# Re-ordering the first phase of a sliding-window attention and FFN kernel

## The chip, the core and the metric

The kernel runs on one core of a Trainium2 chip. The metric is the device time of one execution in microseconds (us), lower is better. Engine names are those of the profile: PE is the matrix engine, PEld its weight loads, DVE the vector engine, ACT the scalar engine, POOL the general engine, SP the engine that only issues DMAs. An "issue" on SP or POOL is the instruction that starts a DMA.

## The reference

Eight batches, eight heads, 576 positions, 64 elements to a head; a causal window of 64 positions. The attention's output becomes 4608 tokens of 512 elements, which go through a multiplicative FFN. All inputs and the output are float32.

```python
scores = scale * np.matmul(q, k.transpose(0, 1, 3, 2))
mask = (rel >= 0) & (rel < window)                # rel = query - key position, window = 64
attn = softmax(where(mask, scores, -1e9))
x = (attn @ v).transpose(0, 2, 1, 3).reshape(B * S, H * D)       # 4608 x 512
a = x @ w1 ; b = x @ w2                           # 512 -> 1024 each
out = ((a * b) @ w3) @ w_out                      # 1024 -> 1024 -> 512
```

## The kernel before

**The attention** is cut into 96 units of work, 12 to a batch (3 stretches of 192 queries, 4 pairs of heads). `tick(u)` issues, in this order, `scores(u)` (2 matmuls into PSUM, one exponential on ACT, then 2 or 4 mask instructions on POOL, lines 262 and 264), every second tick one `transposes` for the next batch, `values(u - 2)` (4 matmuls with V, two logarithms and an exponential on ACT, two multiplications on DVE that write the ring buffer `xT`), and then the loads and casts for later batches that fall on this tick. `LAG = 2` is the distance between the scores of a unit and its values.

**q and k** of a batch are loaded in four DMAs each by SP into a buffer `stage` (4 buffers, shared with the weights), cast to float16 into `k16`/`q16`, and turned by `transposes`: per call 6 transposing matmuls into one PSUM tile `tp` (one buffer) and a copy out of it, by DVE for k, by ACT and then DVE for q. **V** is loaded by DMAs that POOL issues and that cast on the way, as six blocks of 128 rows at rows 0, 64, 128, 256, 320 and 448; neighbouring blocks overlap by 64 rows, so 768 rows are read for 576.

**The FFN** works on 9 groups of 512 tokens. A group is eight `ffn_ab` (8 matmuls of 512 columns, an ACT copy and a DVE multiplication each) and four `ffn_o` (8 matmuls, a DVE copy, a store issued by SP at once). w3 and w_out are multiplied once into `wc_sb` ("the fold"): for each of 8 slices of w3 `fold` casts it on POOL, turns it with 8 transposing matmuls into `tp` and copies it out on DVE, and `fold_mm` multiplies (8 matmuls, one ACT cast).

**The order** is written out by the program: all instructions of one engine run in the order in which the code issues them. First come the loads and transposes of batch 0, the loads and casts of w1 and w2 and the k and q of batch 1; then 14 ticks alone; then the parts of each group, with ticks between them by due times:

```python
need = [12 * B if g == NG - 1 else 12 * g + 4 * -(-(GT - 64 * g) // 192) for g in range(NG)]
...
slots.append((w, lo + (hi - lo) * (i + 1) / len(part) + LAG))
```

`need[g]` is the number of units that group g reads, so a group begins right behind the tick that holds the values of its last unit. Group 0 has the eight fold steps between its `ffn_ab` and its `ffn_o`. At each third of a batch SP copies a row of logarithms to `lnsum`; at the end DVE checks them all, and a branch follows that is not taken.

Of the kernel before, what the change touches and what calls it, by code (L numbers as in the profile page):

```python
# [144 lines left out]
def kernel(  # L145
# [122 lines left out]
    def values(u):  # L268
# [28 lines left out]
        if j == NJ - 1:  # L297
            n = 2 * (3 * b + si)
            nc.sync.dma_start(out=lnsum[n:n + 2, :], in_=y[0:P:D].rearrange("a j n -> a (j n)"))
            del lns[b, si]  # L300

    NU = 12 * B

    def tick(u):
# [4 lines left out]
        if u % 2 == 0 and b + 1 < B:  # L309
            transposes(b + 1, "kq"[r // 6], r % 6 // 2)  # L310
        if 0 <= u - 2 < NU:
            values(u - 2)
        if 3 <= r < 9 and b + 1 < B:
            load_v(b + 1, r - 3)
        if r in (2, 5) and b + 2 < B:
            load_qk(b + 2, "kq"[r == 5])
        if r in (0, 2) and 0 < b + 1 < B:
            cast_qk(b + 1, "q", r // 2, pool_cp)
        if r in (7, 9) and b + 2 < B:
            cast_qk(b + 2, "k", (r - 7) // 2, pool_cp)  # L320
# [32 lines left out]
    w3s = {}
    wo = {}

    def load_w12(dc):
        st = sb.tile([P, 2, 1152], FP32, name="stage", bufs=4)
        for i, src in enumerate((moe_w1, moe_w2)):
            nc.sync.dma_start(out=st[:, i, 0:DF], in_=src[dc * P:(dc + 1) * P, :])
        dve_cp(w1_sb[:, dc, :], st[:, 0, 0:DF])  # L360
        pool_cp(w2_sb[:, dc, :], st[:, 1, 0:DF])

    def load_wo():
        wo[0] = sb.tile([P, 8, DM], FP16, name="ab", bufs=3)
        for half in range(2):
            st = sb.tile([P, 2, 1152], FP32, name="stage", bufs=4)
            for i in range(2):
                e0 = half * 4 + i * 2
                nc.sync.dma_start(out=st[:, i, 0:DF].rearrange("p (e m) -> p e m", e=2),
                                  in_=moe_w_out[e0 * P:(e0 + 2) * P, :].rearrange("(e p) m -> p e m", p=P))  # L370
                pool_cp(wo[0][:, e0:e0 + 2, :], st[:, i, 0:DF].rearrange("p (e m) -> p e m", e=2))

    def load_w3(fc):
        st = sb.tile([P, 2, 1152], FP32, name="stage", bufs=4)
        for i in range(2):
            nc.sync.dma_start(out=st[:, i, 0:DF], in_=moe_w3[(fc + i) * P:(fc + i + 1) * P, :])
        w3s[fc] = st

    def fold(fc):

        st = w3s[fc - fc % 2]
        w3 = sb.tile([P, DF], FP16, name="t2k", bufs=4)
        pool_cp(w3, st[:, fc % 2, 0:DF])  # L383
# [126 lines left out]
```

## Time and profile before

| | us |
|---|---|
| median of 3 runs | 381.17 (381.16 to 382.66) |
| profiled execution, its own time | 382.25 |
| its span, first to last instruction | 380.7 |
| PE busy in the span | 282.8 (74%) |
| DVE, ACT, POOL busy | 209.4, 209.7, 213.1 (55%, 55%, 56%) |
[...]

A busy share is a mean over the whole span. The kernel has a first phase, in which weights, q, k and V have to come in, and a steady phase of one FFN group after the other; the table does not say which of the two a given microsecond of idle PE lies in.

### The profile page before, as it was taken

How to read it: one execution, taken by the hardware profiler on the slowest of the kernel's cores; microseconds unless marked ns; L12 is line 12 of the kernel's file. 1: busy time of each engine (PE TensorE's matmuls, PEld its weight loads, DVE VectorE, ACT ScalarE, POOL GpSimd, SP SyncE). 2: the span in 40 equal slices, each digit the busy share in tenths (PEclk: the TensorE clock that was granted, in tenths of full speed). 3: DMA queues.
4: the chain of work that ended last, by engine and by line, in shares of the span. 5: the costliest groups of instructions: out<-in, count | busy, mean ns of one | idle time of the engine just before them, and what ended most of it. 6: DMA issues, size and time to landing. Idle time of an engine off the chain costs nothing.

```text
span 380.7 us, 5928 instructions
## 1 busy us (share of the span) xinstructions
PE 282.8 (74%) x1922; PEld 163.9 (43%) x1922; DVE 209.4 (55%) x374; ACT 209.7 (55%) x491; POOL 213.1 (56%) x354
## 2 busy tenths in 40 slices
PE   0220555298536688998998998998998998998970
PEld 0120444044323344554554555974554554554430
DVE  7643355146313226666777778575787676555350
ACT  1220476246223234685987888674996996673300
POOL 6022798747462335477699699466889665250000
PEclk9999999999878889999999999999999999999996
DMA  9999989754963203699099499649926723002020
GB/s 173 276 307 197 191 110 216 217 126 38 244 132 113 14 0 115 129 119 195 6 158 213 71 150 197 100 103 181 149 16 122 61 16 112 2 6 108 1 110 10
DMA packets 63753, 45.72 MB, mean 120 GB/s; under 512 B 51888, under 2 KB 51888, under 8 KB 63712
## 3 DMA queue, kind: packets, MB, share of 16 engines
q1 hardware_dynamic: 13792, 38.95, 39.2%
q0 software_dynamic: 49920, 6.29, 28.9%
q8 instruction: 17, 0.28, 0.3%
q14 instruction: 24, 0.20, 0.2%
HBM read 41.94 MB, written 9.44 MB: 135 GB/s over the span
## 4 chain that ended last, share of the span: by engine, by line
PE 67%; POOL 10%; DMA 7%; DVE 6%; ACT 4%; issue 3%; SPq 1%; POOLq 0%; DVEq 0%; ACTq 0%
PE f_ps L337 31%; PE f_ps L347 16%; PE f_ps L394 5%; PE o_ps L280 4%; PE tp L230 4%; PE s_ps L251 4%; DMA stage<-in_moe_w_out_dram 3%; DMA stage<-in_q_dram 3%; POOL pt L262 2%; POOL pt L264 2%; POOL v L218 2%; DMA stage<-in_k_dram 2%; PE tp L386 2%; POOL t2k L383 1%; DVE xT L296 1%
## 5 line engine op out<-in xcount | busy, mean ns | idle before, releaser
L337 PE MATMUL f_ps<-xT,w_sb 128*128 128x512 f16 (+1 forms) x640 | 137.2, 361 | 13.3 <-DVE xT L296 13.1
L262 POOL TENSOR_SCALAR_AFFINE_SELECT pt<-pt 128x512 f16<-128x512 f16 (+2 forms) x128 | 63.2, 494 | 90.0 <-ACT pt L255 89.7
L337 PEld LDWEIGHTS <-w_sb 128*128 128x128 f16 x640 | 60.4, 99 | 67.4 <-issue 19.1
L255 ACT ACTIVATE pt<-s_ps 128x512 f16<-128x512 f32 (+1 forms) x96 | 53.7, 560 | 43.1 <-PE s_ps L251 39.2
L295 DVE TENSOR_TENSOR xT<-o_ps,r 64x192 f16<-64x192 f32 x96 | 33.5, 349 | 63.6 <-ACT r L292 61.3
L264 POOL TENSOR_SCALAR_AFFINE_SELECT pt<-pt 128x512 f16<-128x512 f16 (+2 forms) x128 | 63.1, 493 | 8.7
L341 DVE TENSOR_TENSOR ab<-f_ps,a_sb 128x512 f16<-128x512 f32 x72 | 49.8, 692 | 31.6 <-PE f_ps L337 30.2
L347 PE MATMUL f_ps<-wc_sb,ab 128*128 128x512 f16 x288 | 66.9, 379 | 0.0
L340 ACT COPY a_sb<-f_ps 128x512 f32<-128x512 f32 x72 | 41.3, 574 | 30.3 <-PE f_ps L337 30.3
L280 PE MATMUL o_ps<-pt,v 128*128 128x128 f16 (+1 forms) x384 | 38.0, 224 | 18.1 <-POOL pt L264 14.0
L218 POOL DMA_DIRECT2D v<-in_v_dram x48 | 42.9, 896 | 0.2 <-issue 0.2
L289 ACT ACTIVATE ln_s<-o_ps 64x192 f32<-64x192 f32 x96 | 31.4, 327 | 19.5 <-PE o_ps L280 17.4
L251 PE MATMUL s_ps<-qT,kT 128*128 128x256 f16 x192 | 37.8, 283 | 1.9 <-DVE qT L238 1.9
L347 PEld LDWEIGHTS <-ab 128*128 128x128 f16 x288 | 26.7, 98 | 27.8 <-DVE ab L341 0.4
L280 PEld LDWEIGHTS <-v 128*128 128x128 f16 x384 | 28.2, 102 | 22.4 <-issue 20.0
L238 DVE COPY qT<-tp 64x768 f16<-64x768 f16 x24 | 23.1, 961 | 24.9 <-ACT qT L238 24.9
L292 ACT ACTIVATE r<-ln_s 128x192 f32<-128x192 f32 x96 | 34.8, 363 | 3.0
L296 DVE TENSOR_TENSOR xT<-o_ps,r 64x192 f16<-64x192 f32 x96 | 34.6, 361 | 1.3
L230 PE MATMUL tp<-ident,k 128*128 128x128 f16 x144 | 14.1, 245 | 26.6 <-DVE k L213 13.2
L290 ACT ACTIVATE ln_s<-o_ps 64x192 f32<-64x192 f32 x96 | 30.9, 322 | 1.1
L233 DVE COPY kT<-tp 128x768 f16<-128x768 f16 x24 | 22.8, 951 | 12.4 <-PE tp L230 12.4
L349 DVE COPY t2k<-f_ps 128x512 f32<-128x512 f32 x36 | 24.9, 692 | 7.2 <-PE f_ps L347 6.3
(39 smaller groups left out, 195.3 us busy)
## 6 DMA issues: line engine op xcount, KB each, us to landing
stage<-in_k_dram SPq DMA_DIRECT2D x32, 288.0 KB
stage<-in_q_dram SPq DMA_DIRECT2D x32, 288.0 KB
out_dram<-t2k SPq DMA_DIRECT2D x36, 256.0 KB
stage<-in_moe_w_dram SPq DMA_DIRECT2D x16, 512.0 KB
v<-in_v_dram POOLq DMA_DIRECT2D x48, 128.0 KB, 6.6
stage<-in_moe_w_out_dram SPq DMA_DIRECT2D x4, 512.0 KB
lnsum<-ln_s SPq DMA_DIRECT2D x24, 6.0 KB
```

The costliest lines, as they stand in the source:

```text
L218: nc.gpsimd.dma_start(out=dst, in_=v[b, :, s0:s0 + P, :].rearrange("h s d -> s h d"))
L251: nc.tensor.matmul(s_ps[:, c0:c0 + 2 * n].rearrange("k (a n) -> k a n", a=2), kT[:, j, k0:k0 + P], qT[:, j, :, q0:q0 + n], start=True, sto ...
L255: nc.scalar.activation(pt[:, 0:2 * w], s_ps[:, 0:2 * w], AF.Exp, bias=-SHIFT, scale=scale)
L262: nc.gpsimd.affine_select(out=sl, in_=sl, pattern=[[step, nb], [0, 2], [1, n]], compare_op=ALU.is_ge, fill=0.0, base=off, channel_multipli ...
L264: nc.gpsimd.affine_select(out=sl, in_=sl, pattern=[[-step, nb], [0, 2], [-1, n]], compare_op=ALU.is_ge, fill=0.0, base=63 - off, channel_m ...
L280: nc.tensor.matmul(o_ps[:, a, q0 - q_base:q0 - q_base + n], v16[:, si * 2 + bi, j, a * D:a * D + P], pt[:, c0 + a * n:c0 + a * n + n], sta ...
L292: nc.scalar.activation(r, y[:, j], AF.Exp, scale=-1.0)
L296: nc.vector.tensor_tensor(xs[D:P], o_ps[D:P, 1, :], r[D:P], ALU.mult)
L337: nc.tensor.matmul(d[:, lo:hi], w[:, dc, fc * P:(fc + 1) * P], xT[:, dc, xc:xc + hi - lo], start=(dc == 0 and ci == 0), stop=(dc == 3), sk ...
L340: act_cp(a_sb, a_ps)
L341: nc.vector.tensor_tensor(ab[:, fc, :], b_ps, a_sb, ALU.mult)
L347: nc.tensor.matmul(o_ps, ab[:, fc, t * P:t * P + P], wc_sb[:, fc, :], start=(fc == 0), stop=(fc == 7))
```

## The change

It rewrites what is issued, and where, until group 0 is done, and three things that hold for the whole run.

- **Batch 0.** The two fills of the V buffers with ones move from DVE to POOL. The transposes of batch 0 use three PSUM buffers (`f_ps`) in place of one, and one k copy goes to ACT. V of batch 0 is issued behind a cast of q on POOL. All 12 units of batch 0 run alone, without any instruction of batch 1 between them; w1 and w2 come in 4 DMAs of 1 MB (before: 8 of 0.5 MB) and are cast between the units.
- **Batch 1.** Its k and q are loaded behind w1 and w2, cast after `ffn_ab` 2 of group 0, and turned in two runs of three around `ffn_ab` 4. Its V, and all of w_out and w3, are issued at `ffn_ab` 4; w3 is cast into buffers of its own, partly into an unused part of `xT`. Its 12 units are spread over the last 15 parts of group 0. What batch 2 needs of casts and transposes is put on ticks 19 to 23 (table `second`).
- **V** is read once: 5 loads of 576 rows in all, and three DVE copies to a batch (`copy_v`) fill the overlapping halves.
- **The ticks** of every later group run one further ahead: due times end on `LAG + 1`.
- **Stores** are issued one part later, and the `lnsum` copies (`keep_sums`) four ticks later, the last one behind the last store.

On SP the difference begins so, at its first load (`stage` takes k, q and all weights; `moe_w` is w1 and w2 first and w3 later):

```order
 L204 DMA stage<-in_k_dram 32x2x1152 x4
 L204 DMA stage<-in_q_dram 32x2x1152 x4
-L359 DMA stage<-in_moe_w_dram 128x1024 x8
+L402 DMA stage<-in_moe_w_dram 128x4x512 x4
 L204 DMA stage<-in_k_dram 32x2x1152 x4
 L204 DMA stage<-in_q_dram 32x2x1152 x4
+L314 DMA lnsum<-ln_s 2x768 x2
+L410 DMA stage<-in_moe_w_out_dram 128x4x512 x2
+L415 DMA stage<-in_moe_w_dram 128x2x1024 x4
 L204 DMA stage<-in_k_dram 32x2x1152 x4
-L299 DMA lnsum<-ln_s 2x768
 L204 DMA stage<-in_q_dram 32x2x1152 x4
```

The weights of the fold now stand ahead of the k and q of batch 2 (the last two of the loads shown), and all of w3 in one piece.

On POOL, these rows follow the masks of the last unit of batch 0 in the changed kernel, down to the first mask of batch 1 (`k_469` and `q_472` are the casts of batch 1, `ab` holds w_out and then the first half of w3):

```order
L213 CAST k_469<-stage 128x18x64
L213 CAST q_472<-stage 128x18x64
L220 DMA v_1_86<-in_v_dram 128x8x64 x3
L220 DMA v_1_86<-in_v_dram 64x8x64
L220 DMA v_1_86<-in_v_dram 128x8x64
L521 CAST ab<-stage 128x2048 x2
L425 CAST ab<-stage 128x1024 x4
L271 AFFINE_SELECT pt<-pt 128x256
```

Before, the V issues and casts of batch 1 stood one by one between the masks of batch 0; now they stand together in front of batch 1's first mask.

On PE, the last rows of group 1 before the first matmul of group 2 were these (`pt_1461` is unit 31, the last that group 2 reads; repeated rows and weight loads left out):

```order
L280 MATMUL o_ps_1519<-pt_1420,v16_0_85 128x128
...
L347 MATMUL f_ps_1531<-wc_sb_61,ab_1204 128x512
...
L251 MATMUL s_ps_1543<-qT_0_87,kT_511 128x256
...
L280 MATMUL o_ps_1550<-pt_1461,v16_0_85 128x128
...
L337 MATMUL f_ps_1564<-xT_83,w1_sb_59 128x512
```

and in the changed kernel these (`pt_1431` is unit 31, `pt_1463` unit 32):

```order
L289 MATMUL o_ps_1518<-pt_1431,v16_0_85 128x128
...
L386 MATMUL f_ps_1534<-wc_sb_61,ab_1221 128x512
...
L260 MATMUL s_ps_1545<-qT_0_87,kT_935 128x256
...
L289 MATMUL o_ps_1561<-pt_1463,v16_0_85 128x128
...
L376 MATMUL f_ps_1575<-xT_83,w1_sb_59 128x512
```

The values of unit 31 now have a whole `ffn_o` and a tick between them and the group that reads them. The core of the diff:

```diff
     def load_v(b, c):
-        s0 = VBLK[c]
...
+        vh = v16s[b % 2].rearrange("p c j (a e) -> p c (j a) e", a=2)[:, :, :, 0:D]
+        lo = D if c == 4 else 0
+        s0 = VBLK[c] + lo
+        nc.gpsimd.dma_start(out=vh[lo:P, c], in_=v[b, :, s0:s0 + P - lo, :].rearrange("h s d -> s h d"))
+
+    def copy_v(b, c):
+        vh = v16s[b % 2].rearrange("p c j (a e) -> p c (j a) e", a=2)[:, :, :, 0:D]
+        dve_cp(vh[0:D, c], vh[D:P, c - 1])
+        if c == 1:
+            dve_cp(vh[D:P, 1], vh[0:D, 2])
...
-        tp = ps_t.tile([P, 6, P], FP16, name="tp")
+        tp = ps_f.tile([P, 6, P], FP16, name="f_ps") if early else ps_t.tile([P, 6, P], FP16, name="tp")
...
+            cp = act_cp if early and c == 1 else dve_cp
...
+    def keep_sums(n):
+        b, si = divmod(n, 3)
+        y = lns.pop((b, si))
+        nc.sync.dma_start(out=lnsum[2 * n:2 * n + 2, :], in_=y[0:P:D].rearrange("a j n -> a (j n)"))
...
+    second = {3: [("v", 1, 0)], 4: [("v", 1, 2)], 5: [("v", 1, 3)], 6: [("v", 1, 4)],
+              7: [("v", 1, 5), ("cast", 1, "k", 0)], 8: [("cast", 1, "k", 1)],
+              9: [("t", 1, "k", 0), ("t", 1, "k", 1), ("cast", 1, "q", 0), ("cast", 1, "q", 1), ("load", 2, "k")],
+              10: [("t", 1, "k", 2), ("t", 1, "q", 0), ("copy", 1, 1), ("load", 2, "q")],
+              11: [("t", 1, "q", 1), ("t", 1, "q", 2), ("copy", 1, 4),
+                   ("cast", 2, "k", 0), ("cast", 2, "k", 1)]}
...
+        if (u - LAG - 4) % 4 == 3 and u - LAG - 4 >= 8:
+            keep_sums((u - LAG - 4) // 4)
...
-        nc.sync.dma_start(out=out[r0:r0 + P, :], in_=o_sb)
+        stores.append((r0, o_sb))
...
-    for t in v16s:
-        nc.vector.memset(t.rearrange("p c j (a e) -> p (c j a) e", a=2)[:, :, D:2 * D], 1.0)
...
+    for v16 in v16s:
+        nc.gpsimd.memset(v16.rearrange("p c j (a e) -> p (c j a) e", a=2)[:, :, D:2 * D], 1.0)
+    wst = [load_w12(moe_w1, 0), load_w12(moe_w2, 0)]
...
     for u in range(12 + LAG):
-        tick(u)
+        if u == 2:
+            copy_v(0, 1)
+        if u == 7:
+            copy_v(0, 4)
+        if u == 5:
+            pool_cp(w2_sb[:, :, 0:512], wst[1])
+        if u == 6:
+            dve_cp(w1_sb[:, :, 0:512], wst[0])
+            load_qk(1, "k")
+            load_qk(1, "q")
         if u == 10:
...
+        if u < 12:
+            scores(u)
+        if u >= LAG:
+            values(u - LAG)
...
+            at(3, casts_b1)
+            at(4, load_b1)
+            at(4, lambda: [transposes(1, "k", c) for c in range(3)])
+            at(5, lambda: [transposes(1, "q", c) for c in range(3)])
...
-            slots.append((w, lo + (hi - lo) * (i + 1) / len(part) + LAG))
+            share = max(0, i + 1 - first) / (len(part) - first)
+            slots.append((w, lo + (hi - lo) * share + (LAG + 1) * (i >= first)))
     for w, due in slots:
+        store()
         w()
...
+    store()
+    while u < NU + LAG + 5:
+        tick(u)
+        u += 1
```

`casts_b1` casts k and q of batch 1, one half of each on ACT and one on POOL; `load_b1` issues V of batch 1, the loads of w_out and w3 and the POOL casts shown above; `first` is 5 in group 0 (its first five parts have no tick behind them) and 0 elsewhere.

## Rows read from the trace of the kernel before

**Rows 1.** Busy time in six stretches; per engine us and (x instructions).

```profile
0.00:28.25 28.25, 4.79 (x37) 3.76 (x38) 17.07 (x15) 6.00 (x6) 9.20 (x15) 1.00 1.15 253
28.25:39.40 11.15, 0.47 (x2) 0.10 (x1) 3.31 (x4) 0.49 (x1) 3.72 (x4) 1.00 1.28 198
39.40:76.70 37.30, 17.95 (x119) 12.85 (x120) 15.24 (x31) 20.10 (x52) 31.37 (x52) 1.00 1.10 180
76.70:149.90 73.20, 53.49 (x332) 28.93 (x332) 26.94 (x48) 28.24 (x64) 32.90 (x51) 0.88 0.48 98
149.90:368.60 218.70, 205.96 (x1433) 118.19 (x1430) 143.59 (x272) 154.86 (x368) 135.88 (x236) 1.00 0.63 100
368.60:380.70 12.10, 0.19 (x2) 0.08 (x2) 3.30 (x7) 0.00 (x0) 0.00 (x0) 0.69 0.13 45
```

**Rows 2.** Waits of PE from 150 to 370: total us, times, longest.

```profile
PE f_ps L337 <- DVE xT L296: 12.4, 8, 1.8
```

**Rows 3.** Timeline of the first 40 us: start, us, engine, line, what.

```profile
12.36 0.69 DVE L213 CAST k<-stage 128x1152 f16<-128x1152 f32 x1
...
15.78 1.15 ACT L213 CAST q<-stage 128x1152 f16<-128x1152 f32 x1 [5.11 <-DMA stage<-in_q_dram]
...
18.39 1.04 POOL L361 CAST w_sb<-stage 128x1024 f16<-128x1024 f32 x1 [11.48 <-DMA stage<-in_moe_w_dram]
18.60 1.44 DVE L213 CAST q<-stage 128x1152 f16<-128x1152 f32 x1
...
20.19 0.80 PE L230 MATMUL tp<-ident,q 128*128 128x128 f16 x6 [2.50 <-DVE q L213]
...
22.87 0.80 PE L230 MATMUL tp<-ident,q 128*128 128x128 f16 x6 [1.89 <-DVE qT L238]
...
37.13 2.24 POOL L213 CAST k<-stage 128x1152 f16<-128x1152 f32 x2 [7.32 <-DMA stage<-in_k_dram]
```

**Rows 4.** Two stretches of loads: w1 and w2, then k and q alone; GB/s last.

```profile
14.00:22.00 8.00, 2.39 (x18) 1.83 (x18) 4.38 (x5) 1.96 (x2) 1.76 (x2) 1.00 1.13 354
...
30.00:46.00 16.00, 3.89 (x30) 3.09 (x31) 4.19 (x7) 2.58 (x7) 6.70 (x13) 1.00 1.02 212
```

**Rows 5.** Groups by line and shape: busy us, mean ns, idle before.

```profile
L262 POOL TENSOR_SCALAR_AFFINE_SELECT pt<-pt 128x512 f16<-128x512 f16 x64 | 40.8, 638 | 69.1 <-ACT pt L255 68.9
L255 ACT ACTIVATE pt<-s_ps 128x512 f16<-128x512 f32 x64 | 38.1, 596 | 19.5 <-PE s_ps L251 16.2 <-POOL pt L264 1.4 <-PE o_ps L280 0.8
L292 ACT ACTIVATE r<-ln_s 128x192 f32<-128x192 f32 x96 | 34.8, 363 | 3.0
L289 ACT ACTIVATE ln_s<-o_ps 64x192 f32<-64x192 f32 x96 | 31.4, 327 | 19.5 <-PE o_ps L280 17.4
L238 DVE COPY qT<-tp 64x768 f16<-64x768 f16 x24 | 23.1, 961 | 24.9 <-ACT qT L238 24.9
```

**Rows 6.** Landing of the V loads issued from 0 to 10 us (six).

```profile
L218 POOL DMA_DIRECT2D v<-in_v_dram x6: 881/908/1007, 1.5 to 6.0; - x6
...
DMA to landing us min/median/max: 13.5/24.7/25.5
```

**Rows 7.** The same for two V loads issued from 86 to 92 us.

```profile
DMA to landing us min/median/max: 3.3/3.4/3.4
```

**Rows 8.** The page's DMA queues: the one that V uses.

```profile
q0 software_dynamic: 49920, 6.29, 28.9%
```

**Rows 9.** The chain that ended last, in order of time: start, us, what.

```profile
76.72 4.37 PE f_ps L337 x13
...
117.50 0.45 PE tp L386 x8
117.95 1.74 PE f_ps L394 x8
...
348.29 13.33 PE f_ps L337 x61
361.61 6.92 PE f_ps L347 x32
```

More of the change, by code (lines that the diff above doesn't have):

```diff
@@ L215, in load_v, with transposes @@
     def load_v(b, c):
-        s0 = VBLK[c]
-        dst = v16s[b % 2][:, c].rearrange("p j (a e) -> p (j a) e", a=2)[:, :, 0:D]
-        nc.gpsimd.dma_start(out=dst, in_=v[b, :, s0:s0 + P, :].rearrange("h s d -> s h d"))
+        vh = v16s[b % 2].rearrange("p c j (a e) -> p c (j a) e", a=2)[:, :, :, 0:D]
[7 more added lines that the diff above has]
+            dve_cp(vh[D:P, 1], vh[0:D, 2])
     kTs = {}
-    def transposes(b, which, c):
+    def transposes(b, which, c, early=False):
         if c == 0 and which == "k":
@@ L296, in values, with event @@
         nc.vector.tensor_tensor(xs[D:P], o_ps[D:P, 1, :], r[D:P], ALU.mult)
[L297 to L300, printed above, removed]
     NU = 12 * B
+    LAG = 2
+    VLOADS = {3: 0, 4: 2, 5: 3, 6: 4, 7: 5}
+    def keep_sums(n):
+        b, si = divmod(n, 3)
+        y = lns.pop((b, si))
+        nc.sync.dma_start(out=lnsum[2 * n:2 * n + 2, :], in_=y[0:P:D].rearrange("a j n -> a (j n)"))
+    late = {5: [("load", 2, "q"), ("v", 1, 3)],
[3 rows of a table added]
+            9: [("copy", 1, 1), ("cast", 2, "k", 1)], 11: [("copy", 1, 4)]}
+    second = {3: [("v", 1, 0)], 4: [("v", 1, 2)], 5: [("v", 1, 3)], 6: [("v", 1, 4)],
[5 rows of a table added]
+    def event(b, kind, ahead, *a):
+        if b + ahead >= B:
+            return
+        if kind == "load":
+            load_qk(b + ahead, *a)
+        elif kind == "cast":
+            cast_qk(b + ahead, *a, pool_cp)
+        elif kind == "t":
+            transposes(b + ahead, *a)
+        elif kind == "v":
+            load_v(b + ahead, *a)
+        else:
+            copy_v(b + ahead, *a)
     def tick(u):
@@ L308, in tick @@
             scores(u)
[L309 to L320, printed above, removed]
+        ev = [] if b == 0 else (second if b == 1 else late).get(r, [])
+        for e in ev:
+            if e[0] == "t":
+                event(b, *e)
+        if 12 <= u - LAG < NU:
+            values(u - LAG)
+        if (u - LAG - 4) % 4 == 3 and u - LAG - 4 >= 8:
+            keep_sums((u - LAG - 4) // 4)
+        for e in ev:
+            if e[0] != "t":
+                event(b, *e)
     abs_ = {}
+    stores = []
     def ffn_ab(g, fc):
@@ L350, in ffn_o @@
         r0 = g * GT + t * P
-        nc.sync.dma_start(out=out[r0:r0 + P, :], in_=o_sb)
[L353 to L371, printed above, removed]
@@ L373, in load_w3, with store @@
-    def load_w3(fc):
-        st = sb.tile([P, 2, 1152], FP32, name="stage", bufs=4)
-        for i in range(2):
[L376 to L383, printed above, removed]
+        stores.append((r0, o_sb))
+    def store():
+        while stores:
+            r0, o_sb = stores.pop()
+            nc.sync.dma_start(out=out[r0:r0 + P, :], in_=o_sb)
@@ new lines, in load_w3, with w3_rows, cast_w3 @@
+    def load_w3(n):
+        st = stage().rearrange("p (f n) -> p f n", f=2)
+        nc.sync.dma_start(out=st, in_=moe_w3[n * 256:n * 256 + 256].rearrange("(f p) n -> p f n", p=P))
+        return st
+    def w3_rows(fc):
+        return w3a[:, 2 * fc:2 * fc + 2, :] if fc < 4 else \
+            xT[:, fc - 4, 2 * S:2 * S + DF].rearrange("p (a n) -> p a n", a=2)
+    def cast_w3(n, st, cp):
+        for i in range(2):
+            cp(w3_rows(2 * n + i), st[:, i].rearrange("p (a n) -> p a n", a=2))
```

98 lines of the change are left out of this document (67 added, 31 removed), and 3 rows, old and new, of the table late.

## The prediction

> **What bounds the kernel now.** I first read the busy time of six stretches [rows 1], cut where the chain that ended last changes its character. From 149.9 to 368.6 us PE is busy 206.0 of 218.7 us at full clock: this is the steady phase, and PE bounds it. Ahead of it PE works 4.8 of 28.3, 0.5 of 11.2, 18.0 of 37.3 and 53.5 of 73.2 us, so 73 of 149.9 us are idle there. That is the first phase, and the reader should see that it holds six times the idle time of the rest.
>
> Next came the waits of PE in the steady phase [rows 2]: 12.4 us in 8 waits, one to a group, all of the first `ffn_ab` for the `xT` that DVE writes last. They are nearly the whole 12.7 us of idle PE there.
>
> Then the timeline of the start [rows 3]. The q of batch 0 lands at 15.8. The three runs of q transposes start 2.68 apart (20.19, 22.87), since one PSUM buffer must be emptied by ACT and then DVE before the next run. Unit 0's first score matmul stands at 28.25, where I cut the first stretch, and then next to nothing runs until POOL casts the k of batch 1 at 37.1, which came in behind w1 and w2: tick 0 carries transposes of batch 1. From 39.4 to 76.7 POOL is busy 31.4 of 37.3 us [rows 1], with masks, casts and V issues in turn; from 76.7 to 149.9 PE waits between fold steps.
>
> **The change part by part.** I follow the new order to the moment when group 1 starts (149.9 before), then to the end.
>
> *q of batch 0.* 2.36 MB of k and q at 212 GB/s [rows 4] are 11.1 us, and now no V load runs beside them. The landing lies between 11.1 and the old 15.8; I take 13.3. The two fills that go to POOL (3072 elements each) have no row there; a mask of 512 takes 0.64 [rows 5], so six times that, 3.8 each, is my upper end. They end by 10 and hide behind the landing; longer than 12 in all, and they would push POOL's cast of q.
>
> *Scores of unit 0.* A cast of 1.15 [rows 3], a run of transposes 0.80, ACT's copy 0.8 (what 2.68 leaves beside 0.80, 0.96 and the handovers), then three DVE copies of 0.96 [rows 5], which now follow each other because there are three buffers: 13.3 + 5.9 = 19.2, for 28.25.
>
> *V of batch 0.* Its issues stand on POOL behind the cast of q, so from 14.5 on, 0.91 apart [rows 6]; the second, at 16.3, brings block 2, from which block 1 is copied, and unit 0's values need block 1. Alone such a load lands in 3.4 us [rows 7]; beside k, q and the weights they took 13.5 to 25.5 [rows 6]. So between 19.7 and 41.8. A V load occupies all DMA engines for 0.289 x 380.7 / 48 = 2.3 us [rows 8]. I let the weights go first, as the long landings say: 13.3 + 4.19 MB / 354 GB/s (11.8) [rows 4] + 2 x 2.3, with 0.8 for landing and copy: 30.5. This is the term I know least.
>
> *Twelve units of batch 0.* Per unit ACT needs 0.60 + 2 x 0.33 + 0.36 = 1.62 us [rows 5], POOL 1.3 in masks (0.64 twice); without V issues and batch 1's casts between them ACT sets the pace: 19.4. Two casts of w2 on POOL (2 x 1.04 each [rows 3]) hold masks up for something between 0 and 4.2; I take 1.6. Last multiplications 0.7: group 0 starts at 52.2, for 76.7.
>
> *Parts 0 to 5 of group 0.* Eight `ffn_ab` took 13.33 in one piece [rows 9], 1.67 each; the first 13 matmuls of group 0 took 4.37 [rows 9] where that pace gives 2.84, 1.5 more. Four parts: 60.4. Batch 1 is turned here through the one buffer: k 2 x (0.80 + 0.96) + 0.80, `ffn_ab` 4, then q 3 x 2.68 (`ffn_ab` 5 hides in the last), then scores, exponential and masks of unit 12, 2.0: its values come at 76.5. What POOL has ahead of that first mask (5 V issues, 4.5; w_out, 4.2; half of w3, 4.2, behind its load) ends near 71 if w3's loads, issued at about 60, land in 7 or 8 us; it is covered by the PE chain with 5 us to spare.
>
> *The rest of group 0.* Two `ffn_ab` 3.3, eight fold steps of 1.74 + 0.45 [rows 9] 17.5, four `ffn_o` 6.9 (6.92 [rows 9]). A tick with its share of transposes costs PE 0.63: 206.0 less eight groups of 20.2 is 44.4 for 71 ticks; twelve ticks and two more runs 8.1. Together 35.8. Waits: 1.1 for the first fold's copy; 4.7 on ticks 21 to 23, where six runs go through the buffer that the fold uses too (three copies of 0.96, one of 1.8); 1.2 for POOL's casts of batch 2, since POOL itself has 32 us of work here (masks of 13 units, 5 V issues, 10 casts of 1.04 to 1.15). Group 1 starts at 119.5, where it was 149.9: 30.4 us sooner.
>
> *The steady phase.* 218.7 as before, less the waits. Unit 31's values have an `ffn_o` (1.7) and a tick (0.6) behind them before group 2 needs them, against waits of at most 1.8 [rows 2]: I leave 1.5 of the 12.4, and take off 0.5 for the tick that has already run. 207.3.
>
> *V's DVE copies* (24, of 64x512) have no row. From nothing to the 0.69 of a 128x1152 cast [rows 3], at most 16.6 us over the run on a DVE with 75 us to spare in the steady phase [rows 1]; against them stand eight V issues less on POOL, 7.1. I price them at nothing; the cover would be gone only in the fold's stretch, where POOL is nearly full. There the row speaks against the change: the q cast on DVE took 1.44, the like one of k 0.69, and a POOL cast ran from 18.39 to 19.43 across the former [rows 3], so one of the two engines had waited for the other. Six copies of batches 1 and 2 in that stretch, 0.69 each, would add up to 4.1: 346. [...] By that the sum would be the 346; by the idle time that copies meet elsewhere it stays.
>
> *The tail.* 12.1 as before [rows 1], but the check must now wait for a DMA issued behind the last store: two issues, each under the 0.9 of one on POOL [rows 6], and a landing between nothing and the 3.4 of a V load [rows 7], which is twenty times larger; I take 2.0 and, with the handovers, 3.0 in all. Late stores cost nothing else.
>
> *Sum.* 119.5 + 207.3 + 12.1 + 3.0 = 341.9 as a span. The profiled execution took 382.25 for a span of 380.7, and the median lies 1.08 under it: 341.9 + 1.55 - 1.08 = **342.4**.
>
> **The rivals.** *The fold's stretch takes longer* (348 to 360). [...] Chance 0.20. *The waits at the group starts stay*, because the `xT` chain is held up elsewhere as ACT gets busier: 342.4 + 10.9 = 353. Against it, PE waited for nothing else. 0.08. *V lands early*, near 22 to 24: 334 to 336; the landing of 3.4 alone speaks for it, six landings of 13.5 and more against. With a smoother fold, 329 to 335: 0.13, and 0.02 for still less. *The first phase is bound by the DMAs whatever the order.* Until the fold has its last w3 there are 4.7 MB of k and q (22 us), 10.5 MB of weights (30) and 9 V loads (21): 73 us. That is under the time I give it, so the order does matter; if it did not, 381. 0.02. *Slower:* w3 comes late. Batch 1's first mask stands on POOL behind casts that wait for w3's second load, which is issued near 61 beside the V of batch 1. Past 74, each us of that landing is lost one for one; the longest seen (25.5 [rows 6]) would be at 86.5 and give 355, and slower begins where it takes more than 54 us: 383. 0.03.
>
> **How the numbers follow.** My own case, 335 to 348, has 0.52. The range 329 to 357 leaves out the still faster case, the two last rivals and a part of the first: it reaches down to an early V and up to V's late bound or w3's longest landing. A difference of 0.5% (1.9 us) is about what can be told from none; on the faster side lie all cases but the last two, and a shade for the unknown: faster 0.95, same 0.02, slower 0.03.
>
> **What would show it.** Right: scores of unit 0 near 19, its values near 30, the first `ffn_ab` near 52, values of unit 12 near 76, group 1 near 119, no row of `ffn_ab` waiting for `xT` over 2 us in sum, and the check some 3 us after the last copy. Wrong: V blocks landing past 35, POOL's w3 casts later than 72, a fold stretch over 50 us, or DVE copies that hold masks up.

## The result, and the profile after

The changed kernel takes 345.77 us (median of 4 runs, 345.57 to 346.64), the one before 381.45 beside it (4 runs): a ratio of 0.906, interval 0.904 to 0.909. The profiled execution took 346.64 for a span of 344.8. The forecast was 342.4 (range 329 to 357).

These are the busy times of the new profile in stretches that end at unit 0's first score matmul, the dense start of group 0, the values of unit 12, the first matmul of group 1, PE's last matmul, and the end. [rows 1] has no cut at the values of unit 12, has one at 39.40 that is not made here, and cuts at 149.90 where group 1's first matmul before stands at 149.36. Columns as in [rows 1].

```profile
0.00:20.23 20.23, 4.21 (x37) 3.79 (x38) 10.22 (x11) 5.45 (x6) 11.91 (x14) 1.00 0.94 256
20.23:49.58 29.35, 12.91 (x76) 7.24 (x75) 13.50 (x29) 17.89 (x48) 23.33 (x37) 1.00 1.13 187
49.58:75.81 26.23, 17.38 (x88) 8.59 (x88) 11.12 (x14) 9.30 (x14) 12.64 (x14) 0.87 1.45 281
75.81:126.71 50.90, 40.44 (x301) 23.43 (x300) 25.39 (x48) 26.01 (x61) 33.25 (x54) 0.93 0.54 91
126.71:332.70 205.99, 204.94 (x1426) 118.12 (x1423) 150.76 (x284) 153.29 (x365) 130.78 (x226) 1.00 0.57 101
332.70:344.80 12.10, 0.19 (x2) 0.08 (x2) 3.44 (x7) 0.00 (x0) 0.00 (x0) 0.67 0.14 48
```

The last idle stretch before the steady phase still has 10.5 us without PE work, at a granted clock of 0.93; the steady phase itself has 1.05 left of 12.7. Every wait of PE in it:

```profile
PE f_ps L376 <- DVE ab L380: 0.4, 2, 0.2
PE f_ps L376 <- DVE t2k L388: 0.4, 1, 0.4
```

The eight waits for `xT` of [rows 2] are gone. On PE's timeline the first phase reads as follows (start, us, what, and in brackets the idle time before and what ended it):

```profile
15.77 2.10 PE L238 MATMUL f_ps<-ident,q 128*128 128x128 f16 x18 [4.06 <-POOL q L213]
20.23 0.80 PE L260 MATMUL s_ps<-qT,kT 128*128 128x256 f16 x4 [2.35 <-DVE qT L247]
...
26.09 0.29 PE L289 MATMUL o_ps<-pt,v 128*128 128x128 f16 x1 [4.33 <-DMA v<-in_v_dram]
27.57 0.40 PE L289 MATMUL o_ps<-pt,v 128*128 128x64 f16 x3 [1.18 <-DVE v L226]
...
67.13 0.80 PE L238 MATMUL tp<-ident,q 128*128 128x128 f16 x6 [2.88 <-DVE qT L247]
69.82 0.80 PE L238 MATMUL tp<-ident,q 128*128 128x128 f16 x6 [1.89 <-DVE qT L247]
70.41 3.62 PE L376 MATMUL f_ps<-xT,w_sb 128*128 128x512 f16 x8
...
84.01 0.91 PE L432 MATMUL tp<-ident,ab 128*128 128x128 f16 x8 [2.69 <-DVE t2k L434]
84.71 3.31 PE L440 MATMUL f_ps<-ab,t2k 128*128 128x512 f16 x8
...
88.69 1.89 PE L440 MATMUL f_ps<-ab,t2k 128*128 128x512 f16 x8
...
117.51 0.49 PE L238 MATMUL tp<-ident,q 128*128 128x128 f16 x6 [2.10 <-DVE qT L247]
...
118.07 3.39 PE L386 MATMUL f_ps<-wc_sb,ab 128*128 128x512 f16 x8
```

Two things are to be seen. Unit 0 waits for V, not for its scores. And three groups of eight matmuls of 512 columns (at 70.4, 84.7, 118.1) take 3.3 to 3.6 us where others take 1.89: the granted clock there was 0.51, 0.57 and 0.53 (1.00 in the groups of 1.89 at 62.0 and 88.7), each behind a wait of 1.9 to 2.7 us for a copy of DVE.

Where the 35.9 us of span came from: group 1 starts at 126.71 in place of 149.36 (its first matmul in both), 22.7; from there to PE's last matmul 206.0 in place of 219.2, 13.2; behind it 12.1 in both, where two things cancel (see the tail below).

### The profile page after: what moved, and what is told of

It is laid out like the page before. It is cut to its first block, busy times and chain, and to the rows that moved or that the text cites. A ratio compares the mean times of both kernels' runs of the same rounds, so it can differ in the third digit from the quotient of the medians.

```text
span 344.8 us, 5950 instructions
## 1 busy us (share of the span) xinstructions
PE 280.1 (81%) x1922; PEld 161.2 (47%) x1922; DVE 214.4 (62%) x393; ACT 211.9 (61%) x493; POOL 211.9 (61%) x343
## 3 DMA queue, kind: packets, MB, share of 16 engines
q1 hardware_dynamic: 14656, 38.95, 41.6%
q0 software_dynamic: 37504, 4.72, 26.5%
## 4 chain that ended last, share of the span: by engine, by line
PE 68%; DVE 8%; POOL 8%; DMA 6%; ACT 4%; issue 3%; SPq 1%; DVEq 0%; ACTq 0%; POOLq 0%
PE f_ps L376 33%; PE f_ps L386 18%; PE o_ps L289 5%; PE tp L238 4%; PE s_ps L260 4%; DMA v<-in_v_dram 3%; PE f_ps L440 3%; DMA stage<-in_q_dram 3%; POOL pt L271 2%; POOL pt L273 2%; DVE kT L242 1%; DVE ab L380 1%; DVE qT L247 1%; ACT pt L264 1%; DVE xT L305 1%
## 5 line engine op out<-in xcount | busy, mean ns | idle before, releaser
L271 POOL TENSOR_SCALAR_AFFINE_SELECT pt<-pt 128x512 f16<-128x512 f16 (+2 forms) x128 | 65.3, 510 | 70.4 <-ACT pt L264 70.0
L376 PEld LDWEIGHTS <-w_sb 128*128 128x128 f16 x640 | 61.3, 99 | 56.1 <-issue 7.5
L273 POOL TENSOR_SCALAR_AFFINE_SELECT pt<-pt 128x512 f16<-128x512 f16 (+2 forms) x128 | 64.4, 503 | 8.8
L386 PE MATMUL f_ps<-wc_sb,ab 128*128 128x512 f16 x288 | 68.6, 385 | 0.0
L379 ACT COPY a_sb<-f_ps 128x512 f32<-128x512 f32 x72 | 41.3, 574 | 27.2 <-PE f_ps L376 27.2
L289 PEld LDWEIGHTS <-v 128*128 128x128 f16 x384 | 27.5, 101 | 22.6 <-issue 6.9
L220 POOL DMA_DIRECT2D v<-in_v_dram x40 | 34.3, 862 | 1.7 <-DVE xT L305 1.1
L260 PEld LDWEIGHTS <-kT 128*128 128x128 f16 x192 | 19.5, 104 | 22.7 <-issue 4.9
L247 DVE COPY qT<-tp 64x768 f16<-64x768 f16 x21 | 20.2, 961 | 9.9 <-ACT qT L247 9.6
L242 DVE COPY kT<-tp 128x768 f16<-128x768 f16 x21 | 20.0, 951 | 4.2 <-PE tp L238 4.2
```

The costliest lines, as they stand in the source:

```text
L220: nc.gpsimd.dma_start(out=vh[lo:P, c], in_=v[b, :, s0:s0 + P - lo, :].rearrange("h s d -> s h d"))
L260: nc.tensor.matmul(s_ps[:, c0:c0 + 2 * n].rearrange("k (a n) -> k a n", a=2), kT[:, j, k0:k0 + P], qT[:, j, :, q0:q0 + n], start=True, sto ...
L271: nc.gpsimd.affine_select(out=sl, in_=sl, pattern=[[step, nb], [0, 2], [1, n]], compare_op=ALU.is_ge, fill=0.0, base=off, channel_multipli ...
L273: nc.gpsimd.affine_select(out=sl, in_=sl, pattern=[[-step, nb], [0, 2], [-1, n]], compare_op=ALU.is_ge, fill=0.0, base=63 - off, channel_m ...
L289: nc.tensor.matmul(o_ps[:, a, q0 - q_base:q0 - q_base + n], v16[:, si * 2 + bi, j, a * D:a * D + P], pt[:, c0 + a * n:c0 + a * n + n], sta ...
L376: nc.tensor.matmul(d[:, lo:hi], w[:, dc, fc * P:(fc + 1) * P], xT[:, dc, xc:xc + hi - lo], start=(dc == 0 and ci == 0), stop=(dc == 3), sk ...
```

## The experiments

The times in the table are of one profiled execution of each kernel; medians and ratios are of its 4 to 6 executions, and the ratios are to the kernel before, run beside them. The spans of one kernel's executions lie 1.0 to 5.4 us apart (343.8 to 344.8 for the changed kernel, 341.1 to 345.2 in experiment 6, 380.3 to 385.7 for the kernel before beside it), so 2 us of a single span tell little. What repeats is the time from group 1 on: 217.7 to 218.2 in the seven profiles whose steady phase and tail are the same (changed, 4, 6, 7, 8, 10, 12). The changed kernel was not run again beside the experiments; experiment 4, whose times agree with its own to 0.3, has a ratio of 0.902 (0.899 to 0.905) there. Times at which things start, in us:

| | scores of unit 0 | values of unit 0 | first ffn_ab | values of unit 12 | group 1 | group 1 to end | span |
|---|---|---|---|---|---|---|---|
| before | 28.25 | 41.89 | 74.61 | 81.43 | 149.36 | 231.3 | 380.7 |
| changed | 20.23 | 26.09 | 47.47 | 75.81 | 126.71 | 218.1 | 344.8 |
| 1 old due times | 20.34 | 26.26 | 47.62 | 76.76 | 125.04 | 233.0 | 358.0 |
| 2 before, extra tick | 27.55 | 42.62 | 75.17 | 79.80 | 150.91 | 213.9 | 364.8 |
| 3 sums at once | 20.07 | 25.99 | 47.35 | 75.77 | 126.64 | 215.7 | 342.3 |
| 4 stores at once | 20.47 | 26.36 | 47.75 | 76.01 | 126.66 | 218.1 | 344.8 |
| 5 V in six blocks | 20.46 | 26.34 | 47.38 | 74.73 | 123.96 | 216.3 | 340.3 |
| 6 one `tp` | 24.08 | 26.28 | 47.61 | 75.99 | 125.19 | 217.8 | 343.0 |
| 7 V first | 20.30 | 22.31 | 47.55 | 74.67 | 125.56 | 218.1 | 343.7 |
| 8 batch 1, three buffers | 20.12 | 26.16 | 47.43 | 68.64 | 119.38 | 218.2 | 337.6 |
| 9 = 3 + 5 + 8 | 20.30 | 26.15 | 47.18 | 72.12 | 123.19 | 213.9 | 337.1 |
| 10 weights behind V | 20.48 | 22.49 | 41.58 | 76.24 | 128.37 | 217.7 | 346.1 |
| 11 all | 20.67 | 22.68 | 41.78 | 67.90 | 118.84 | 214.0 | 332.8 |
| 12 busy matmuls | 20.10 | 26.13 | 47.39 | 73.19 | 122.49 | 218.2 | 340.7 |

**Experiments 1 and 2, the extra tick.** Experiment 1 takes it out of the changed kernel:

```diff
-            slots.append((w, lo + (hi - lo) * share + (LAG + 1) * (i >= first)))
+            slots.append((w, lo + (hi - lo) * share + LAG * (i >= first)))
```

> The changed kernel with the due times of before (the extra tick taken back, all else kept). My theory: the extra tick alone removed the eight waits of the groups' first matmuls for xT, so they come back, 12 us of PE waits for DVE's xT in the steady phase, and the time is 356 to 358 (345.8 + 11 or so). Rival: the waits went because the ring is fed sooner by the rest of the change (late stores, eight V issues less, masks sooner): PE's waits for xT stay under 3 us in sum and the time is 346 to 348.

Experiment 2 puts it alone into the kernel before:

```diff
-            slots.append((w, lo + (hi - lo) * (i + 1) / len(part) + LAG))
+            slots.append((w, lo + (hi - lo) * (i + 1) / len(part) + LAG + 1))
```

> The kernel before with one edit: due times end on LAG + 1. My theory: the eight waits of 12.4 us shrink to less than 2, nothing else moves, and the time is 369 to 372. Rival: with the old order of loads and V issues one tick is not enough or pushes other waits into its place: 376 to 381.

Experiment 1: 360.58 us, ratio 0.938 (0.935 to 0.942), above the 356 to 358 expected. Its executions took 2.7 to 4.0 us more than their spans, those of all other kernels 1.5 to 1.9; why is open. PE's waits from 125 us on are back, to the tenth those of [rows 2]:

```profile
PE f_ps L376 <- DVE xT L305: 12.4, 8, 1.8
```

Experiment 2: 366.86 us, ratio 0.954 (0.949 to 0.959), below the 369 to 372 expected, and no wait of PE in its steady phase:

```profile
150.91:354.95 204.04, 204.04 (x1426) 117.94 (x1423) 143.07 (x269) 152.70 (x365) 134.44 (x231) 1.00 0.68 108
354.95:364.80 9.85, 0.19 (x2) 0.08 (x2) 3.35 (x7) 0.00 (x0) 0.00 (x0) 0.71 0.17 58
```

My theory holds both ways round; the rival (the ring is fed sooner by the rest) falls. The tick is worth 13.5 to 13.7 us at PE's last matmul: 368.60 became 354.95 here, and taking it out moved 332.70 to 346.20. 12.4 of it are the waits; the rest is what a wait costs besides, since it cuts the first 16 matmuls of a group in two. The kernel before, at group 1, and experiment 2:

```profile
149.36 0.81 PE L337 MATMUL f_ps<-xT,w_sb 128*128 128x512 f16 x3
151.77 2.97 PE L337 MATMUL f_ps<-xT,w_sb 128*128 128x512 f16 x13 [1.60 <-DVE xT L296]
...
150.91 3.62 PE L337 MATMUL f_ps<-xT,w_sb 128*128 128x512 f16 x16
```

That is 0.16 more in 0.81 + 2.97 than in one piece, an estimated 1.3 for eight groups. From group 1 on it looks like more (219.2 became 204.0), because group 1 starts 1.6 later: one tick's work, 0.7 us of PE, now stands ahead of it, and the rest is within the scatter. And 2.3 of the 15.9 us of span lie behind PE's last matmul (12.1 and 9.85), where the edit changes nothing. The changed kernel's 206.0 is 2.0 above that of the old kernel with the tick: something else in the change costs (experiment 5).

**Experiment 3, the lnsum copies at once,** with the last one ahead of the last stores.

```diff
-        if (u - LAG - 4) % 4 == 3 and u - LAG - 4 >= 8:
-            keep_sums((u - LAG - 4) // 4)
+        if (u - LAG) % 4 == 3 and 12 <= u - LAG < NU:
+            keep_sums((u - LAG) // 4)
```

> The changed kernel with the lnsum copies issued right behind the values of their third, as before, so that the last of them is not behind the last store. My theory: the check starts some 0.7 us behind the last copy out of PSUM in place of 2.9, and the end comes 2.2 us sooner: 343.5. Rival: what follows the check ends at a fixed distance behind PE's last matmul, 12.1 us in both kernels, whatever the check waits for; then the time stays 345.8, and the stretch from the last DVE cast to the end grows from 6.0 to about 8.3 us.

342.79 us, ratio 0.892 (0.889 to 0.894). The check in the changed kernel (last copy, check, last cast):

```profile
332.74 0.69 DVE L388 COPY t2k<-f_ps 128x512 f32<-128x512 f32 x1 [1.04 <-PE f_ps L386]
335.65 0.95 DVE L558 TENSOR_TENSOR chk<-lnsum 48x768 f32<-48x768 f32 x1 [2.23 <-DMA lnsum<-ln_s]
...
338.64 0.14 DVE L567 CAST bad_i<-tp 1x1 int32<-1x1 f32 x1 [0.28 <-PE tp L566]
```

and in experiment 3:

```profile
332.33 0.69 DVE L388 COPY t2k<-f_ps 128x512 f32<-128x512 f32 x1 [1.03 <-PE f_ps L386]
332.94 0.94 DVE L558 TENSOR_TENSOR chk<-lnsum 48x768 f32<-48x768 f32 x1
...
335.91 0.15 DVE L567 CAST bad_i<-tp 1x1 int32<-1x1 f32 x1 [0.28 <-PE tp L566]
```

The check starts 0.6 behind the last copy in place of 2.9, and from PE's last matmul to the end it takes 10.0 in place of 12.1: the wait was paid almost in full, and the rival (a fixed distance behind PE) falls.

**Experiment 4, the stores at once.**

```diff
-        stores.append((r0, o_sb))
+        nc.sync.dma_start(out=out[r0:r0 + P, :], in_=o_sb)
```

> The changed kernel with each store issued right behind its copy out of PSUM, in place of one part later; the lnsum copies stay late. My theory: SP has nothing behind the store that is urgent, so nothing changes: 345 to 346.5, the end included. Rival: a store that waits for its copy holds up the loads of k and q behind it on SP, POOL's casts of them come late and PE waits for them at the transposes: 348 or more.

346.35 us, ratio 0.902 (0.899 to 0.905), span 344.8: no column of the table differs by over 0.3. No gain or cost of late stores can be told.

**Experiment 5, V as six blocks.**

```diff
-        lo = D if c == 4 else 0
-        s0 = VBLK[c] + lo
-        nc.gpsimd.dma_start(out=vh[lo:P, c], in_=v[b, :, s0:s0 + P - lo, :]...)
+        s0 = VBLK[c]
+        nc.gpsimd.dma_start(out=vh[:, c], in_=v[b, :, s0:s0 + P, :]...)
...
-    VLOADS = {3: 0, 4: 2, 5: 3, 6: 4, 7: 5}
+    VLOADS = {3: 0, 4: 1, 5: 2, 6: 3, 7: 4, 8: 5}
...
     def copy_v(b, c):
-        dve_cp(vh[0:D, c], vh[D:P, c - 1])
-        if c == 1:
-            dve_cp(vh[D:P, 1], vh[0:D, 2])
+        if b > 1 and c == 1:
+            load_v(b, c)
```

> The changed kernel with V read as six blocks of 128 rows again, block 1 and 4 loaded in place of copied (24 DVE copies less, 8 V loads and POOL issues more, 0.9 us each). My theory: V read once is worth nothing in the time, but block 1 no longer needs block 2 and a copy in the first ticks, and the sixth load puts up to 2.3 us on the queue of batch 0: unit 0's values within 1.5 us of 27.6 and 345 to 347. Rival 1: the first phase is short of DMA time, and one load more for batches 0 and 1 costs 2 to 5 us: 348 to 351. [...]

342.14 us, ratio 0.892 (0.888 to 0.897): my theory falls, and rival 1 with it: the time is under both, so the copies cost. The span is 4.5 shorter: 1.1 ahead of unit 12, 1.7 in the fold's stretch, 1.8 behind. The 1.7 is all PE's busy time (40.4 to 38.8: one slow group, 3.40 us at 115.5, where the changed kernel has two, 3.31 and 3.39), and experiment 6, which keeps the copies, has the same 38.8 in a stretch of the same 49.2. So it is not shown to be the copies' price; the 1.1 and the 1.8 are. The groups of the copies in the changed kernel (busy us, mean ns, idle before):

```profile
L224 DVE COPY v<-v 64x512 f16<-64x512 f16 x16 | 7.1, 446 | 6.4 <-DMA v<-in_v_dram 5.9
L226 DVE COPY v<-v 64x512 f16<-64x512 f16 x8 | 4.8, 594 | 1.1 <-DMA v<-in_v_dram 0.9
```

and two of them on DVE's timeline, ahead of the copy of qT that PE waits for:

```profile
64.75 0.29 DVE L224 COPY v<-v 64x512 f16<-64x512 f16 x1
65.07 1.01 DVE L226 COPY v<-v 64x512 f16<-64x512 f16 x1
66.12 0.96 DVE L247 COPY qT<-tp 64x768 f16<-64x768 f16 x1
```

A copy took 0.29 where POOL was quiet (the two of experiment 7 below) or had not yet begun (64.75), and 1.01 behind the start of POOL's cast of w3 at 64.78. What lengthens it beside the cast no run shows. ACT's half of qT was done at 65.1, so the copy of qT starts 1.0 late, and PE waits 2.88 for it where it waits 1.89 in experiment 5. Of that 1.0, 0.7 is the stretching beside POOL and the rest the copies' place in DVE's queue, ahead of what PE waits for. Two other profiles have the same copies at this place. In experiment 4 POOL casts from 64.64 on, the copies take 1.12 and 1.01, and PE waits 3.71 for qT. In experiment 7 the cast comes only at 65.41, and PE waits 2.15 behind these:

```profile
64.38 0.29 DVE L224 COPY v<-v 64x512 f16<-64x512 f16 x1
64.70 0.29 DVE L226 COPY v<-v 64x512 f16<-64x512 f16 x1
```

So here the place in the queue costs 0.3 us, and what POOL casts beside the copies 0 to 1.6 more. Over the run the 24 copies took 11.9 us, where 24 of 0.29 are 7.0. They cost in the steady phase too: with six blocks it takes 204.04, PE never idle, as in experiment 2; the changed kernel takes 206.0.

**Experiments 6 and 7, what unit 0 waits for.** Experiment 6 sends batch 0's transposes through the one `tp`, 7 issues V ahead of everything else on POOL.

```diff
-            transposes(0, which, c, early=True)
+            transposes(0, which, c)
```

> The changed kernel with batch 0's transposes through the one PSUM buffer tp, as before. The q runs start 2.7 apart in place of about 1, so unit 0's scores come near 23.6 in place of 20.2. My theory: the values of unit 0 wait for V until 26.1 to 27.6 anyway, and 23.6 + 2.0 for exponential and masks is within that, so the time stays within 1 us of 345.8: the three buffers bought nothing. Rival: each us of the first score is lost one for one: 349.

```diff
+    for c in VLOADS.values():
+        load_v(0, c)
     wst = [load_w12(moe_w1, 0), load_w12(moe_w2, 0)]
...
-    for c in VLOADS.values():
-        load_v(0, c)
     wst += [load_w12(moe_w1, 1), load_w12(moe_w2, 1)]
```

> The changed kernel with batch 0's V issued on POOL ahead of its cast of q (right behind the fills), so 4 to 8 us sooner. My theory: V lands sooner (20 to 23) and q a little later (15 to 16, as in the kernel before, where both were under way at once); scores near 22, values near 24, and the time 343 to 344.5. Rival: V starves beside the loads of k, q and weights however early it is issued, as before (landings of 13.5 to 25.5 us), lands at 26 or later, and the time is 345.5 to 348.

Experiment 6: 344.95 us, ratio 0.899 (0.894 to 0.904). Scores 3.9 us later, values 0.2: my theory holds, the three buffers of batch 0 bought nothing. (Its span is 1.8 shorter; the slow groups of eight matmuls fell elsewhere, one at 61.1 (3.05 us) and none at 84.7, so less than 2 us at group 1's start tells nothing by itself.) Experiment 7: 345.83 us, ratio 0.902 (0.898 to 0.907): the rival holds. DVE's copies of V in experiment 7:

```profile
20.86 0.29 DVE L224 COPY v<-v 64x512 f16<-64x512 f16 x1 [0.61 <-DMA v<-in_v_dram]
27.30 0.29 DVE L226 COPY v<-v 64x512 f16<-64x512 f16 x1 [6.16 <-DMA v<-in_v_dram]
```

Block 0 landed 5 us sooner, but block 2, though issued 9 us earlier (7.5 and 16.7), at 27.3 as in the changed kernel (27.2). From issue to landing block 2 and those behind it took 19.4 to 20.2 us here and 10.5 to 10.8 in the changed kernel. That the loads of the weights hold them back is shown by experiment 10, where all five took 8.5 to 9.2.

**Experiment 10, the weights behind V,** with V first as in 7. SP waits in a small DMA that reads V's last block; the casts of w1 and w2 move back to fit.

```diff
-    wst = [load_w12(moe_w1, 0), load_w12(moe_w2, 0)]
...
+    held = const.tile([P, 64], FP16)
+    nc.sync.dma_start(out=held[D:P], in_=v16s[0][D:P, 5, 0, 0:64])
+    wst = [load_w12(w, half) for half in range(2) for w in (moe_w1, moe_w2)]
```

> The changed kernel with batch 0's V issued ahead of the cast of q, and w1 and w2 issued only when the last V block has landed (SP waits in a small DMA that reads it); their casts are moved back to fit (first halves at unit 10, second halves behind unit 13). Nothing else changes. My theory: V starves as long as the weights' loads are under way, and with the weights behind it unit 0's values stand at 22 to 23 and the first ffn_ab at 43 to 45 in place of 47.5; the time is 341.5 to 344. Rival: the weights, or the k and q of batch 1 behind them, now come late, the first ffn_ab or the transposes of batch 1 wait for them, and the time is 346 to 352.

349.03 us, ratio 0.911 (0.907 to 0.915). At its place the theory holds (values of unit 0 at 22.49, first `ffn_ab` at 41.58, 5.9 sooner), in the time the rival does: k and q of batch 1 now land late, ACT's cast of q holds up its copy for `ffn_ab`, and PE waits in the transposes of batch 1. The second wait below stands behind DVE's copies of batch 1's V, which waited 1.4 for their load and took 1.57 and 0.29:

```profile
56.08 0.80 PE L238 MATMUL tp<-ident,k 128*128 128x128 f16 x6 [4.83 <-DVE kT L242]
...
67.43 0.80 PE L238 MATMUL tp<-ident,q 128*128 128x128 f16 x6 [4.76 <-DVE qT L247]
```

**Experiment 8, batch 1's transposes through three buffers.**

```diff
-            at(4, lambda: [transposes(1, "k", c) for c in range(3)])
-            at(5, lambda: [transposes(1, "q", c) for c in range(3)])
+            at(4, lambda: [transposes(1, "k", c, early=True) for c in range(3)])
+            at(5, lambda: [transposes(1, "q", c, early=True) for c in range(3)])
```

> The changed kernel with the transposes of batch 1 through the three f_ps buffers in place of tp (the middle k copy goes to ACT by the same switch). My theory: between 58 and 75 us PE's chain through the one buffer sets when unit 12 has its values; with three it gains 4 to 5 us there, POOL's masks (idle 7.9 us ahead of the first one) can follow, group 1 starts at 122 in place of 126.7 and the time is 340.5 to 343. Rival: POOL's w3 casts or V of batch 1 are next in line and the gain is under 1 us: 345 to 346.5.

340.65 us, ratio 0.888 (0.883 to 0.892). Unit 12 is 7.2 us sooner, group 1 7.3, the span 7.2. My theory holds, with more than I expected: the `ffn_ab` behind the q runs now takes 1.90 us, at 64.97, where it took 3.62. POOL's rows show what is next: the mask waits 0.54 where it waited 7.88.

```profile
65.14 2.02 POOL L425 CAST ab<-stage 128x1024 f16<-128x1024 f32 x2 [1.36 <-DMA stage<-in_moe_w_dram]
67.71 0.41 POOL L271 TENSOR_SCALAR_AFFINE_SELECT pt<-pt 128x256 f16<-128x256 f16 x1 [0.54 <-ACT pt L264]
```

**Experiments 9 and 11, the edits together.** 9 is 3, 5 and 8; 11 adds 10, with batch 0's V still in five loads.

> The changed kernel with three edits at once: the lnsum copies at once, V in six blocks, batch 1's transposes through three buffers. Their profiled spans were 2.5, 4.5 and 7.2 us under that of the changed kernel (344.8). My theory: the three sit at different places (behind the last matmul; DVE's queue in the fold's stretch and the steady phase; PE's wait for the one buffer between 57 and 75 us), so they add up: a span near 330.6 and a time of 331 to 333. Rival: copies and buffers pay for the same wait of the q transposes for DVE's qT, so 1 to 3 us are counted twice: 333.5 to 336.

> The three edits together and the weights behind V (batch 0 keeps five V loads and copies, the later batches read six blocks). My theory: another 2 to 4 us less than the three edits alone: 328 to 330. Rival: with batch 1's transposes shortened, what comes next in line is the landing of batch 1's k and q or of w3, which the held weights make later: no better than the three edits alone.

Experiment 9: 339.11 us, ratio 0.885 (0.881 to 0.889), slower than both the theory (331 to 333) and the rival (333.5 to 336), and not to be told from experiment 8 alone. Behind group 1 the gains of 3 and 5 add up (213.9). Ahead of it 3.8 us of experiment 8's are gone, but not as the rival had it: unit 12's values wait 5.45 for a mask, which stands behind casts of w3 that wait for their load.

```profile
66.33 2.02 POOL L422 CAST ab<-stage 128x1024 f16<-128x1024 f32 x2 [6.73 <-DMA stage<-in_moe_w_dram]
69.21 2.02 POOL L422 CAST ab<-stage 128x1024 f16<-128x1024 f32 x2 [0.86 <-DMA stage<-in_moe_w_dram]
71.19 0.41 POOL L268 TENSOR_SCALAR_AFFINE_SELECT pt<-pt 128x256 f16<-128x256 f16 x1
...
72.12 0.27 PE L286 MATMUL o_ps<-pt,v 128*128 128x128 f16 x1 [5.45 <-POOL pt L270]
```

Two edits make w3 late: the sixth V load of batch 1 ahead of it, and a lnsum copy that now waits on SP ahead of w_out's load (issued at 48.68; 44.53 in experiment 8). The profiles of 3 and 5 have each of them alone. POOL's first cast of w3 starts at 61.81 in the changed kernel, at 64.97 in 3 and at 63.85 in 5: the lnsum copies put it off by 3.2 us, the sixth load by 2.0. With both, in experiment 9, it is 4.6 behind experiment 8's 61.70. In 3 and 5 alone it cost nothing, since PE's chain through the one buffer held unit 12 up for longer. Experiment 11: 335.47 us, ratio 0.873 (0.870 to 0.877), the fastest of all, though not the 328 to 330 expected. Its span is 4.3 under that of 9, all of it ahead of group 1; the two differ in the weights behind V, which alone made the time longer, and in batch 0's five loads. Unit 12's values still wait 3.51 for a mask, and group 1's start is only 0.5 ahead of experiment 8's.

**Experiment 12, matmuls that nothing reads,** in four of PE's waits.

```diff
+    def warm(n):
+        t = ps_f.tile([P, DM], FP32, name="f_ps")
+        for _ in range(n):
+            nc.tensor.matmul(t, ident16, w1_sb[:, 0, 0:512], start=True, stop=True)
...
     def transposes(b, which, c, early=False):
+        if which == "q" and (b == 1 and c or b == 2 and c == 2):
+            warm(7)
...
                     w3Ts[0] = fold_t(0)
+                    warm(9)
```

> The changed kernel with matmuls that nothing reads (9 of 512 columns between the first two fold transposes, 7 each ahead of three q runs that wait for qT) put where PE waits; the rest is unchanged. My theory: the three groups of eight matmuls at half speed in the fold's stretch and ahead of it (3.62 at 70.4, 3.31 at 84.7, 3.39 at 118.1, where 1.89 is the rule) are half-speed because PE sat idle before them; with the gaps filled they take 1.9 each, group 1 starts 4 to 5 us sooner and the time is 341 to 342.5. Rival: the low clock has another cause, or the added matmuls stand ahead of work that was ready and hold it up by as much: 345 to 348.

343.32 us, ratio 0.893 (0.889 to 0.897), just over the 341 to 342.5 expected. The three groups took 1.89 us each, and one that had taken as much (at 107.2 in the changed kernel) now took 3.27:

```profile
69.22 1.89 PE L378 MATMUL f_ps<-xT,w_sb 128*128 128x512 f16 x8
...
81.83 1.89 PE L447 MATMUL f_ps<-ab,t2k 128*128 128x512 f16 x8
...
102.88 3.27 PE L447 MATMUL f_ps<-ab,t2k 128*128 128x512 f16 x8
...
115.42 1.89 PE L388 MATMUL f_ps<-wc_sb,ab 128*128 128x512 f16 x8
```

Group 1 starts 4.2 us sooner. The theory holds as far as these three groups took 1.89 us with those waits filled. The group at 102.9 stands behind waits of only 0.7, 1.1 and 0.8 us, which the changed kernel has too (0.7, 1.1 and 0.8 ahead of its fast group at 107.2); why it slowed there is open.

## Why the prediction was right

The total was right to 1%, and so were the main steps of the mechanism, but the closeness is in part luck, errors that cancel: against the forecast's 341.9, the span of 344.8 is -0.7 up to unit 12, +7.9 to group 1, -1.3 in the steady phase and -3.0 in the tail.

- **q and scores of batch 0:** q landed at 13.95 (forecast 13.3), scores at 20.2 (19.2); POOL's cast of q took 1.73 beside one of DVE. But this term did not enter the sum: V hides it (experiment 6).
- **V of batch 0:** that the weights go first was right (experiments 7 and 10). The two V loads behind them did not take 2.3 us each in a row: unit 0 went on at 27.6, not 30.5, and group 0's dense start was at 49.6, not 52.2.
- **Parts 0 to 5 of group 0:** values of unit 12 at 75.8 (76.5), set by PE's chain through the one buffer, as forecast (experiment 8). POOL's cover was 7.9 us, not 5.
- **The fold's stretch is the mis-sized term:** 43.0 from the values of unit 12 to group 1 in the forecast, 50.9 measured; I had this as a rival with 0.20. PE was busy 40.4 us where I counted 36, 2.9 of it two slow groups (3.31 and 3.39 us for 1.89), and idle 10.5 where I counted 7.0.
- **V's DVE copies:** that they cost nothing is a step that failed. Six blocks take 1.1 off ahead of unit 12, most of it the 1.01 for 0.29 beside POOL's cast, and 1.8 off behind group 1's start; the 1.7 in between comes with the copies kept as well (experiment 6). I had weighed 4.1 for them, in the fold's stretch, and set it aside; 2.9 is what the profiles show, at other places. That one of the two engines had waited for the other, as I read the row of the q cast, no run shows; the runs show how long a copy takes with POOL quiet and beside a cast.
- **The steady phase:** 206.0 for 207.3. The tick removes the waits altogether, where I had left 1.5, and some 1.3 of cut runs with them (experiments 1 and 2); the copies take 2.0 back.
- **The tail:** the check's wait is 2.2 us, and experiment 3 shows that it costs 2.1 behind PE's last matmul (I had 3.0). Yet the stretch is 12.1 as before: from the last cast (`bad_i`) to the end took 8.4 in the profile of before (372.28 to 380.7) and 6.0 here. In experiment 2, the kernel before with other due times, it is 6.1. What the 2.4 were is open; that they made up for the check's wait is luck.
- **The rivals:** V neither came so early nor so late as they had it. That DMAs bind the first phase whatever the order got 0.02: in that form it is wrong, but each later version ran into the next load (V, then k and q of batch 1, then w3). w3's late landing, my way to slower, had a margin here, and held unit 12 up by 5.45 us in experiment 9.
- **Sums:** the 73 us idle ahead of group 1 are six times the steady phase's 12.7, but only three times the rest, which has 11.9 in the tail too; and the terms up to group 1 add up to 119.3, not 119.5. Nothing hangs on either.

Not tried: batch 0's units with batch 1's work between them as before, so that the share of that one part in the 22.7 us stays open.

## What to carry to other kernels

Follow the whole chain to the point where the stretch ends: the edits that looked strongest at their place (scores 4 us sooner, V's issue 9 us sooner, the first `ffn_ab` 6 us sooner) gave no gain that can be told alone; the last one was part of a gain only with the buffer behind it moved too (experiments 10 and 11). A wait at the start of each group can be removed by one more step of distance, and that edit can be tested alone. A copy is not free because its engine has time to spare; ask what stands behind it in that engine's queue, and what runs beside it on another engine (0.29 us became 1.01 beside POOL's cast). Two edits that each cost nothing alone can hold the next thing up together, so run them together before adding their gains.
